# The end of the first attention and the first expert unit: blocks made as the values come, six products in another order

## The chip, the cores and the metric

The kernel runs on one core of one Trainium2 chip. The metric is the device time of one execution in microseconds (us). A core has TensorE (PE, with its weight loads shown apart as PEld), VectorE (DVE), ScalarE (ACT), GpSimd (POOL) and SyncE (SP, which here issues most of the DMAs). Each engine works through its own queue in order; semaphores tie the queues together. [...]

## The reference

```python
# attention: B=4, H=8, S=768, D=64; n_global=8, n_local=96
scores = scale * np.matmul(q, k.transpose(0, 1, 3, 2))
rel = pos[:, None] - pos[None, :]
keep = is_global | ((rel >= 0) & (rel < n_local))
scores = np.where(keep, scores - slopes * dist, -1e9)
a = softmax(scores)
attn_out = np.matmul(a, v)
# mixture: N = B*S = 3072 rows, model width 512, E=4 experts, F=1024
x = attn_out.transpose(0, 2, 1, 3).reshape(B * S, H * D)
p = domain_probs / (domain_probs.sum(-1, keepdims=True) + 1e-09)
for e in range(E):
    h = np.maximum(x @ w1[e], 0.0)
    out += p[:, e:e + 1] * (h @ w2[e])
```

All is fp32.

## The kernel before

**Precision.** A number is split into a high part, rounded to the fast matmul type, and a low part, the rest. A product is then three matmuls: high by high, low by high, high by low. The high part is mostly a ScalarE copy (`high`), the low part a subtraction on VectorE or GpSimd (`rest`).

**The mixture.** Its work is cut into units: for each of the 4 batches, 4 experts and 4 groups of 256 hidden columns, so 16 units in a batch. A unit has a first half, `first(i)` (x times w1), and a second half, `second(i)` (h times w2, six row tiles of 128, summed up over the units in `acc`). The first half multiplies 2x2 blocks by a scheme with seven products instead of eight (Winograd's form of Strassen): the weights give A11, A12, A22 and the sums S1 to S4, and x gives B11, B21, B22 and the sums T1 to T4. B11 and B12 are the first and second 384 rows of the first half of the model width, B21 and B22 those of the second half; a block spans two of the four pairs of heads (k = 0, 1 and k = 2, 3). T3 = B22 - B12, T2 = T3 + B11, T1 = B22 - T2, T4 = B21 - T2, made in place in x. Each product is six matmuls of 128x384 (two halves of the depth, three of high and low) into one PSUM tile `pm` of a pool of four. The results are joined by VectorE additions; ScalarE takes the relu as the high part of h and VectorE makes the low part (`late`, `work_late`).

**The attention.** Four pairs of heads per batch, in the order 0, 2, 1, 3, each with six row tiles of 128. One yield of `attention` is a step: the scores of one tile, the softmax of the tiles before, the turn (four transposes) of the third last, and after every third tile `weigh`, the px product with the values, whose result ScalarE copies to x. In the first batch these steps are numbered n = 0 to 27: scores come in steps 0 to 23, the last turn is in step 26, and x gets its halves of a pair in steps 6 and 9 (pair 0), 12 and 15 (pair 2), 18 and 21 (pair 1), 24 and 27 (pair 3).

**Chores.** Weights are loaded and prepared by generators that are moved one piece on after each step (`work_chores`). `load_w1` issues a load to the one buffer raw1, waits `lead` pieces, lets GpSimd make the four sums, waits `hold` pieces, and then makes four slices, a ScalarE copy and a GpSimd subtraction each. `load_w2` does the same in two slices without sums. In the first batch `keep` writes the prepared weights to DRAM, and later batches fetch them from there. `blocks` makes the B and T blocks of x, in steps too: for k = 0 during the first attention from step 17 on (pairs 0 and 2), with the low parts on GpSimd, and for k = 1 (pairs 1 and 3) after it.

**Order.** While `Ordered.on` is true, each engine's instructions stand in the order in which the program emits them. That holds for the first attention and, until `done == ONSTEPS`, for the first half of unit 0. After that a planner, which weighs costs and due times, sets the order on each engine, and the next batch's attention is spread between the units' pieces.

Of the kernel before, what the change touches and what calls it, by code (L numbers as in the profile page):

```python
# [18 lines left out]
P = 128  # L19
# [6 lines left out]
def f32(ap):  # L26
    return ap.bitcast(F32)
# [158 lines left out]
def attn_moe_kernel(ctx: ExitStack, tc, q, k, v, n_global, n_local, domain_probs, w1, w2, out):  # L186
# [25 lines left out]

    BIASES = ((0, 1), (0, 3), (1, 0), (1, 2))

    ONSTEPS = 7

    PL = P + NGLOB
    fast = main.enter_context(tc.tile_pool(name="fast", bufs=1))
# [75 lines left out]
    def mixture():  # L294

        sy.dma_start(prob, domain_probs.rearrange("(t p) e -> p t e", p=P))
        yield
        psumm = fast.tile([P, NT, 1], F32, name="psumm")
        ve.reduce_sum(psumm, prob, axis=AX.X)
        ve.tensor_scalar_add(psumm, psumm, 1e-9)  # L300
        ve.reciprocal(psumm, psumm)
        for e in range(E):
            ve.tensor_mul(prob[:, :, e : e + 1], prob[:, :, e : e + 1], psumm)
# [176 lines left out]
    xs = {}  # L480
# [116 lines left out]
    def blocks(b, ks=(0, 1), low=ve):  # L597

        lo, hi = ks[0], ks[-1] + 1
        b11, b12 = xs[b][:, lo:hi, :HALF], xs[b][:, lo:hi, HALF:]
        b21, b22 = xs[b][:, 2 + lo : 2 + hi, :HALF], xs[b][:, 2 + lo : 2 + hi, HALF:]

        def high(name, src):
            if lo == 0:
                xb[name] = bp.tile([P, 2, 2, HALF], F32R, name=f"x{name}")
            ac.copy(xb[name][:, 0, lo:hi], src)

        def rest(eng, name, src):  # L610
            eng.tensor_tensor(xb[name][:, 1, lo:hi], src, f32(xb[name][:, 0, lo:hi]), op=ALU.subtract)

        high("B11", b11)
        high("B22", b22)
        ve.tensor_sub(b12, b22, b12)
        rest(po, "B22", b22)
        yield 1
        rest(low, "B11", b11)
        ve.tensor_add(b11, b12, b11)
        high("T2", b11)  # L620
        yield 1
        rest(low, "T2", b11)
        ve.tensor_sub(b22, b22, b11)
        high("T1", b22)
        yield 1
        rest(low, "T1", b22)
        high("T3", b12)
        yield 1
        rest(po, "T3", b12)
        high("B21", b21)  # L630
        ve.tensor_sub(b11, b21, b11)
        yield 1
        rest(po, "B21", b21)
        high("T4", b11)
        yield 1
        rest(low, "T4", b11)
        yield 1


    NPR = FF // (2 * P)  # L640
    units = [(b, e, g) for b in range(B) for e in range(E) for g in range(NPR)]
# [7 lines left out]
    def keep(i, n):  # L649

        if (i, n) in waiting:
            key, dst = waiting.pop((i, n))
            kept[key] = dp.tile(list(dst.shape), F32R, name="kept_{}_{}_{}".format(*key))
            sy.dma_start(f32(kept[key]), f32(dst))
# [6 lines left out]
    def load_w1(i, wait=0, lead=5, hold=2):  # L661


        if i >= len(units):
            return
        b, e, g = units[i]
        if b > 0:
            wts[(i, 1)] = fetch("w1s", (e, g, 1), [P, 2, 7, 2, P], lambda t: {
                name: t[:, :, n] for n, name in enumerate(("A11", "A12", "A22", "S1", "S2", "S3", "S4"))
            })  # L670
            return
        for _ in range(wait):
            yield 1
        raw = rp.tile([P, KT, 2 * P], F32, name="raw1")
        sy.dma_start(raw, w1[e, :, g * 2 * P : (g + 1) * 2 * P].rearrange("(a p) f -> p a f", p=P))
        for _ in range(lead):
            yield 1
        a11, a21 = raw[:, 0:2, :P], raw[:, 0:2, P:]
        a12, a22 = raw[:, 2:4, :P], raw[:, 2:4, P:]
        sums = rp.tile([P, 4, 2, P], F32, name="sums")  # L680
        s1, s2, s3, s4 = (sums[:, n] for n in range(4))
        po.tensor_add(s1, a21, a22)
        po.tensor_sub(s2, s1, a11)
        po.tensor_sub(s3, a11, a21)
        po.tensor_sub(s4, a12, s2)
        for _ in range(hold):
            yield 1
        dst = wp.tile([P, 2, 7, 2, P], F32R, name="w1s")
        wts[(i, 1)] = {name: dst[:, :, n] for n, name in enumerate(("A11", "A12", "A22", "S1", "S2", "S3", "S4"))}
        for sl, src in (  # L690
            (slice(0, 2), raw[:, :, :P].rearrange("p (n a) f -> p n a f", n=2)),
            (slice(2, 3), a22.rearrange("p (n a) f -> p n a f", n=1)),
            (slice(3, 5), sums[:, 0:2]),
            (slice(5, 7), sums[:, 2:4]),
        ):
            ac.copy(dst[:, 0, sl], src)
            po.tensor_tensor(dst[:, 1, sl], src, f32(dst[:, 0, sl]), op=ALU.subtract)
            yield 1
        waiting[(i, 1)] = (e, g, 1), dst

    def load_w2(i, lead=7):

        if i >= len(units):
            return
        b, e, g = units[i]
        if b > 0:
            wts[(i, 2)] = fetch("w2s", (e, g, 2), [P, 2, 2, DM], lambda t: t)
            return
        raw = rp.tile([P, 2, DM], F32, name="raw2")
        sy.dma_start(raw, w2[e, g * 2 * P : (g + 1) * 2 * P, :].rearrange("(a p) m -> p a m", p=P))  # L710
        for _ in range(lead):
            yield 1
        dst = wp.tile([P, 2, 2, DM], F32R, name="w2s")
        wts[(i, 2)] = dst
        for f in range(2):
            ac.copy(dst[:, 0, f], raw[:, f])
            po.tensor_tensor(dst[:, 1, f], raw[:, f], f32(dst[:, 0, f]), op=ALU.subtract)
            yield 1
        waiting[(i, 2)] = (e, g, 2), dst

    hs = {}

    def product(i, a, x):

        pm = ps_mm.tile([P, 512], F32, name="pm")
        m = 0
        for kt in range(2):
            for wi, xi in ((0, 0), (1, 0), (0, 1)):
                te.matmul(
                    pm[:, :HALF], wts[(i, 1)][a][:, wi, kt, :], xb[x][:, xi, kt, :], start=(m == 0), stop=(m == 5)  # L730
                )
                m += 1
        return pm
# [3 lines left out]
    def work_late():  # L737

        while late:
            lo, src, hi = late.pop()  # L740
            ve.scalar_tensor_tensor(lo, src, 0.0, f32(hi), op0=ALU.max, op1=ALU.subtract)

    def first(i):

        h = hp.tile([P, 2, 2, S], F32R, name="h")
        hs[i] = h

        def relu(f, c, src):
            hi, lo = h[:, 0, f, c * HALF : (c + 1) * HALF], h[:, 1, f, c * HALF : (c + 1) * HALF]
            ac.activation(hi, src, AF.Relu)  # L750
            late.append((lo, src, hi))

        def add(out, pm, other):
            ve.tensor_add(out, pm[:, :HALF], other)
            work_late()

        def last(pm, other):

            add(pm[:, :HALF], pm, other)
            return pm[:, :HALF]  # L760

        p1, u, vv = (up.tile([P, HALF], F32, name=n) for n in ("p1", "u", "vv"))
        keep(i, 1)
        pm = product(i, "A11", "B11")
        ac.copy(p1, pm[:, :HALF])
        yield
        add(u, product(i, "S2", "T2"), p1)
        yield
        add(vv, product(i, "S1", "T1"), u)
        yield  # L770
        pm = product(i, "S3", "T3")
        add(u, pm, u)
        relu(1, 1, last(pm, vv))
        yield
        relu(0, 0, last(product(i, "A12", "B21"), p1))
        yield
        relu(0, 1, last(product(i, "S4", "B22"), vv))
        yield
        relu(1, 0, last(product(i, "A22", "T4"), u))
        yield  # L780
# [33 lines left out]
    def work_chores():  # L814
        for c in list(chores):
            if next(c, 0) == 0:
                chores.remove(c)

    bp = main.enter_context(tc.tile_pool(name="bp", bufs=1))
    Ordered.on = True  # L820
    with ExitStack() as start_stack:
        A = Pools(start_stack, "start", st=1, kd=2, qd=2, nat=2, natv=3, pb=4, ps=2, pt=3, px=1, early=True)
        for n, _ in enumerate(attention(0, A, early=True)):
            if n == 9:
                chores += [load_w1(0, lead=2), load_w2(0, lead=3)]
            if n == 18:
                chores.append(load_w1(1, lead=2, hold=3))
            if n == 2 * NQT + 5:
                chores.append(blocks(0, (0,), po))
            work_chores()  # L830
        mix = mixture()
        next(mix)
    Ordered.on = False
    hp = main.enter_context(tc.tile_pool(name="hp", bufs=2))
    up = main.enter_context(tc.tile_pool(name="up", bufs=1))
    op = main.enter_context(tc.tile_pool(name="op", bufs=1))
    ps_mm = main.enter_context(tc.tile_pool(name="ps_mm", bufs=4, space=PSUM))
    A = Pools(main, "att", st=1, kd=1, qd=1, nat=1, natv=1, pb=2, ps=2, pt=2, px=0, early=False)
# [3 lines left out]
    per = E * NPR  # L842
    count, span = NPAIR * (6 + NQT) + 5, (13 * per - 12) * 0.97
    Ordered.on = True
    chores.append(blocks(0, (1,)))
    for _ in range(2):
        work_chores()
    for b in range(B):
        att = attention(b + 1, A) if b + 1 < B else iter(())
        emitted = done = 0  # L850
# [67 lines left out]
```

## Time and profile before

| | |
|---|---|
| runs | 1203.69 us median of 3 (1201.08 to 1203.73) |
| profiled execution | 1202.66 us |
| its span, first to last instruction | 1200.9 us |
| mean granted PE clock | 0.993 |
| busy: PE, DVE, ACT, POOL | 1174.0, 824.1, 494.7, 210.7 us |
| first attention's last px product ends | 68.69 us |
| unit 0's second half starts on PE | 87.97 us |

Rows of the profile name tiles with buffer numbers left out: ps are scores, pb probabilities, pt transposes, px the weighted values, pm the products of the mixture, xB and xT the blocks B and T, w1s and w2s the prepared weights. All these instructions stand under one line, 42, because one helper emits them, so they are told apart by tile. An arrow from an engine and tile behind a row names what ended the idle time before it.

### The profile page before, as it was taken

Reading aid. Unit: us, or ns where it says so; the run is one execution under the profiler, and the core shown is the slowest. Engines: PE = TensorE matmul, PEld = TensorE weight load, DVE = VectorE, ACT = ScalarE, POOL = GpSimd, SP = SyncE. Lnnn points to the kernel's source line nnn. Section 1 sums busy time; section 2 is a strip of 40 time slices with the busy share of each in tenths; the row PEclk is TensorE's granted clock in tenths of the full one; section 3 lists DMA queues with packets and bytes.
Section 4 is the critical chain, followed back from the end, with each engine's and each line's share of the span. In section 5 each row is a group of like instructions: output and inputs, shape, how many; then the busy total and the mean of one; then the engine's idle time right before and its main releaser. Section 6 shows DMA issues by size and latency. Waiting matters only on the chain.

```text
span 1200.9 us, 18119 instructions
## 1 busy us (share of the span) xinstructions
PE 1174.0 (98%) x6624; PEld 1045.0 (87%) x6624; DVE 824.1 (69%) x1858; ACT 494.7 (41%) x1268; POOL 210.7 (18%) x222
## 2 busy tenths in 40 slices
PE   7889999999999999999999999999999999999997
PEld 5677889989889989989888989989898999999996
DVE  7776567667678767676668767676666766666665
ACT  6865655565643444444342434444443211111110
POOL 4645655645440000000002000000000000000000
PEclk9899999999999999999999999999999999999999
DMA  7456777787878567565746757574663655544532
GB/s 169 119 198 214 259 288 245 288 292 234 325 253 265 191 198 239 187 220 176 240 169 205 248 186 228 196 231 163 219 206 132 245 194 193 187 178 181 190 132 90
DMA packets 122704, 251.39 MB, mean 209 GB/s; under 512 B 83184, under 2 KB 91376, under 8 KB 106224
## 3 DMA queue, kind: packets, MB, share of 16 engines
q1 hardware_dynamic: 118864, 243.87, 61.1%
q10 hardware_dynamic: 3744, 6.30, 1.4%
q8 instruction: 54, 0.88, 0.3%
q14 instruction: 42, 0.34, 0.1%
HBM read 174.11 MB, written 52.43 MB: 189 GB/s over the span
## 4 chain that ended last, share of the span: by engine, by line
PE 88%; DMA 3%; ACT 2%; issue 2%; POOL 2%; DVE 1%; SPq 1%; POOLq 0%; ACTq 0%; DVEq 0%
PE pm L42 77%; PE pt L42 7%; PE ps L42 4%; DMA raw<-in_moe_w_dram 2%; POOL sums L42 1%; PE px L42 1%; POOL w2s L42 1%; ACT pb L42 1%; SPq L42 1%; DMA qd<-st_q 1%; DMA q<-in_q_dram 0%; ACT xT L42 0%; DVE x L42 0%; ACT xB L42 0%; ACT h L42 0%
## 5 line engine op out<-in xcount | busy, mean ns | idle before, releaser
L42 PE MATMUL pm<-w2s,h 128*128 128x512 f32 x2304 | 551.7, 393 | 4.5 <-DVE h L42 4.5
L42 PEld LDWEIGHTS pm<-w2s,h 128*128 128x128 f32 x2304 | 426.1, 188 | 92.5 <-DVE h L42 6.3
L42 DVE SCALAR_TENSOR_TENSOR acc<-pm,prob,acc 128x512 f32<-128x512 f32 x360 | 268.2, 749 | 148.8 <-PE pm L42 146.5
L42 PE MATMUL pm<-xT,w1s 128*128 128x384 f32 x1536 | 296.7, 338 | 0.2 <-ACT xT L42 0.2
L42 PEld LDWEIGHTS pm<-xT,w1s 128*128 128x128 f32 x1536 | 267.8, 189 | 2.5 <-issue 1.4
L42 PE MATMUL pm<-xB,w1s 128*128 128x384 f32 x1152 | 226.8, 338 | 1.8 <-DVE xB L42 1.5
L42 PEld LDWEIGHTS pm<-xB,w1s 128*128 128x128 f32 x1152 | 201.3, 188 | 7.0 <-DVE xB L42 1.8
L42 ACT ACTIVATE h<-pm 128x384 fp32r<-128x384 f32 x256 | 124.8, 491 | 177.7 <-DVE pm L42 174.3
L42 DVE SCALAR_TENSOR_TENSOR h<-pm,h 128x384 fp32r<-128x384 f32 x256 | 140.9, 552 | 13.1 <-ACT h L42 9.5
L42 ACT ACTIVATE pb<-pb,nmax 128x256 f32<-128x256 f32 (+1 forms) x192 | 93.1, 487 | 95.3 <-DVE nmax L42 94.6
L42 ACT COPY p<-pm 128x384 f32<-128x384 f32 x64 | 30.7, 479 | 191.1 <-PE pm L42 182.0
L42 POOL COPY vg<-v 32x768 f32<-32x768 f32 x16 | 13.2, 828 | 498.6 <-DMA v<-in_v_dram 435.9
L42 DVE TENSOR_TENSOR u<-pm,p 128x384 f32<-128x384 f32 x64 | 35.6, 556 | 73.4 <-PE pm L42 53.5
L42 DVE CUSTOM_DVE_ANT_0 pb<-ps,nbias 128x256 f32<-128x256 f32 (+1 forms) x192 | 71.7, 397 | 10.5 <-PE ps L42 5.7
L42 ACT COPY pT<-pt 128x512 f32<-128x512 f32 (+1 forms) x96 | 52.6, 548 | 58.1 <-PE pt L42 57.8
L42 DVE TENSOR_TENSOR pm<-pm,vv 128x384 f32<-128x384 f32 x128 | 71.7, 560 | 1.6 <-PE pm L42 1.4
L42 ACT ACTIVATE pb<-pb,zsum 128x256 f32<-128x256 f32 (+1 forms) x144 | 63.3, 485 | 18.0 <-DVE zsum L42 18.0
L42 PE MATMUL pt<-ident,pb 128*128 128x128 f32 x352 | 58.3, 283 | 2.7 <-DVE pb L42 1.5
L42 PEld LDWEIGHTS pt<-ident,pb 128*128 128x128 f32 x352 | 42.2, 143 | 15.4 <-ACT pb L42 3.6
L42 DVE TENSOR_TENSOR vv<-pm,u 128x384 f32<-128x384 f32 x64 | 35.7, 557 | 27.1 <-PE pm L42 26.2
L42 DVE TENSOR_TENSOR u<-pm,u 128x384 f32<-128x384 f32 x64 | 35.7, 557 | 25.1 <-PE pm L42 24.4
L42 POOL TENSOR_TENSOR w2s<-raw,w2s 128x512 fp32r<-128x512 f32 x32 | 41.0, 1296 | 57.6 <-ACT w2s L42 57.6
(88 smaller groups left out, 887.3 us busy)
## 6 DMA issues: line engine op xcount, KB each, us to landing
w1s<-kept SPq DMA_DIRECT2D x48, 1792.0 KB, 7.4
w2s<-kept SPq DMA_DIRECT2D x48, 1024.0 KB, 4.9
kept<-w1s SPq DMA_DIRECT2D x16, 1792.0 KB, 9.5
qd<-st_q SPq DMA_DIRECT2D x96, 192.0 KB, 4.7
raw<-in_moe_w_dram SPq DMA_DIRECT2D x32, 512.0 KB, 5.6
kept<-w2s SPq DMA_DIRECT2D x16, 1024.0 KB, 6.7
v<-in_v_dram SPq DMA_DIRECT2D x16, 384.0 KB, 3.4
out_dram<-acc ACTq DMA_DIRECT2D x24, 256.0 KB, 3.9
```

The lines of the kernel that those rows point to most:

```text
L42: ins = fn(*args, **kwargs)
```

## The change

- Step 9 begins w1 and w2 of unit 0 as before, but w2's two slices come in steps 14 and 15 instead of 12 and 13.
- w1 of unit 1 begins in step 17 instead of 18 and is held one step less: its slices come in steps 21 to 24 instead of 23 to 26.
- The blocks for k = 1 come from a new generator, `last_blocks`. B11 is split after step 19 (its low part on GpSimd), B21 after step 26 (on VectorE); after the attention come B22, T2, T1, T3, T4, with all low parts but T3's on VectorE. Before, B21's and B22's were GpSimd's too.
- Unit 0's first product, A11·B11, is issued after step 25, into a PSUM tile of the scores' pool (`opening`), and its result is copied to p1. `keep`, the write of unit 0's w1 to DRAM, goes with it.
- The other six products of unit 0 come in the order A12·B21, S4·B22, S2·T2, S1·T1, S3·T3, A22·T4. S4·B22 stays in its PSUM tile until S1·T1 has been added. Before, it was A11·B11, S2·T2, S1·T1, S3·T3, A12·B21, S4·B22, A22·T4.
- `ONSTEPS` is 6 instead of 7, as unit 0's first half has one piece less. After the attention one round of chores runs before unit 0 instead of two.

```diff
-    ONSTEPS = 7
+    ONSTEPS = 6
...
+    def last_blocks():
+        b11, b12, b21, b22 = (
+            xs[0][:, k : k + 1, s] for k in (1, 3) for s in (slice(0, HALF), slice(HALF, S))
+        )
+        def high(name, src):
+            ac.copy(xb[name][:, 0, 1:2], src)
+        def rest(eng, name, src):
+            eng.tensor_tensor(xb[name][:, 1, 1:2], src, f32(xb[name][:, 0, 1:2]), op=ALU.subtract)
+        high("B11", b11)
+        rest(po, "B11", b11)
+        yield 1
+        high("B21", b21)
+        rest(ve, "B21", b21)
+        yield 1
+        high("B22", b22)
+        ve.tensor_sub(b12, b22, b12)
+        ve.tensor_add(b11, b12, b11)
+        rest(ve, "B22", b22)
+        high("T2", b11)
+        rest(ve, "T2", b11)
+        yield 1
+        ve.tensor_sub(b22, b22, b11)
+        high("T1", b22)
+        rest(ve, "T1", b22)
+        yield 1
+        high("T3", b12)
+        rest(po, "T3", b12)
+        yield 1
+        ve.tensor_sub(b11, b21, b11)
+        high("T4", b11)
+        rest(ve, "T4", b11)
+        yield 1
...
+    def opening(A):
+        ups.append(sums_of_products())
+        keep(0, 1)
+        pm = product(0, "A11", "B11", A.ps.tile([P, 512], F32, name="ps0"))
+        ac.copy(ups[0][0], pm[:, :HALF])
...
+        if i == 0:
+            p1, u, vv = ups.pop()
+            relu(0, 0, last(product(i, "A12", "B21"), p1))
+            yield
+            pm4 = product(i, "S4", "B22")
+            yield
+            add(u, product(i, "S2", "T2"), p1)
+            yield
+            add(vv, product(i, "S1", "T1"), u)
+            relu(0, 1, last(pm4, vv))
+            yield
+            pm = product(i, "S3", "T3")
+            add(u, pm, u)
+            relu(1, 1, last(pm, vv))
+            yield
+            relu(1, 0, last(product(i, "A22", "T4"), u))
+            yield
+            return
...
             if n == 9:
-                chores += [load_w1(0, lead=2), load_w2(0, lead=3)]
-            if n == 18:
-                chores.append(load_w1(1, lead=2, hold=3))
+                chores += [load_w1(0, lead=2), load_w2(0, lead=5)]
             if n == 2 * NQT + 5:
-                chores.append(blocks(0, (0,), po))
+                chores += [load_w1(1, lead=2, hold=2), blocks(0, (0,), po)]
             work_chores()
+            if n == 3 * NQT + 1:
+                last = last_blocks()
+                next(last)
+            if n == 4 * NQT + 1:
+                opening(A)
+            if n == 4 * NQT + 2:
+                next(last)
...
-    chores.append(blocks(0, (1,)))
-    for _ in range(2):
-        work_chores()
+    chores.append(last)
+    work_chores()
```

More of the change, by code (lines that the diff above doesn't have):

```diff
@@ L721, in attn_moe_kernel, with product @@
     hs = {}
-    def product(i, a, x):
-        pm = ps_mm.tile([P, 512], F32, name="pm")
+    def product(i, a, x, pm=None):
+        if pm is None:
+            pm = ps_mm.tile([P, 512], F32, name="pm")
         m = 0
@@ L741, in work_late, with sums_of_products @@
             ve.scalar_tensor_tensor(lo, src, 0.0, f32(hi), op0=ALU.max, op1=ALU.subtract)
+    ups = []
+    def sums_of_products():
+        return [up.tile([P, HALF], F32, name=n) for n in ("p1", "u", "vv")]
+    def opening(A):
[3 more added lines that the diff above has]
+        ac.copy(ups[0][0], pm[:, :HALF])
     def first(i):
@@ L760, in last @@
             return pm[:, :HALF]
-        p1, u, vv = (up.tile([P, HALF], F32, name=n) for n in ("p1", "u", "vv"))
+        if i == 0:
[16 more added lines that the diff above has]
+            return
+        p1, u, vv = sums_of_products()
         keep(i, 1)
@@ L819, in attn_moe_kernel @@
     bp = main.enter_context(tc.tile_pool(name="bp", bufs=1))
+    up = main.enter_context(tc.tile_pool(name="up", bufs=1))
     Ordered.on = True
@@ L834, in attn_moe_kernel @@
     hp = main.enter_context(tc.tile_pool(name="hp", bufs=2))
-    up = main.enter_context(tc.tile_pool(name="up", bufs=1))
     op = main.enter_context(tc.tile_pool(name="op", bufs=1))
```

## The prediction

> **What bounds the kernel now.** I read the page's busy times first, then busy times by stretch of time. In each stretch row stand the length, the busy time of PE (with instruction count), PEld, DVE, ACT and POOL, the granted PE clock, the DMA share and GB/s.
>
> ```profile
> span 1200.9 us, 18119 instructions
> PE 1174.0 (98%) x6624; PEld 1045.0 (87%) x6624; DVE 824.1 (69%) x1858; ACT 494.7 (41%) x1268; POOL 210.7 (18%) x222
> ...
> 0.00:73.00 73.00, 59.88 (x418) 39.73 (x418) 52.83 (x291) 55.15 (x166) 41.59 (x57) 0.93 0.50 131
> 73.00:100.00 27.00, 25.19 (x125) 22.67 (x126) 20.85 (x44) 10.21 (x23) 12.52 (x13) 0.94 0.71 215
> 100.00:130.00 30.00, 27.09 (x147) 24.28 (x147) 18.23 (x47) 17.98 (x48) 19.52 (x20) 1.00 0.88 302
> 160.00:200.00 40.00, 38.02 (x215) 34.60 (x216) 25.48 (x58) 24.57 (x65) 26.68 (x28) 1.00 0.81 273
> ```
>
> TensorE is the bound: it idles 26.9 us in all, 13.1 of them before 73 us (the first attention and its end, which the change edits) and 6.7 in the three later stretches shown (1.8, 2.9, 2.0). Whatever makes the expert stage begin earlier ends the program earlier by as much, unless a later gap grows.
>
> **Part 1, w2's preparation two steps later.** Times next to steps (one step is one yield of the first attention, some 1.8 us) come from the timelines: start, duration, engine, instruction, idle time before it and its releaser.
>
> ```profile
> 34.37 0.52 ACT L42 ACTIVATE early_q<-pt 128x384 f32<-128x384 f32 x1
> 37.13 0.62 ACT L42 CAST w2s<-raw 128x512 fp32r<-128x512 f32 x1 [2.24 <-DMA raw<-in_moe_w_dram]
> ...
> 36.01 0.73 POOL L42 TENSOR_TENSOR sums<-raw 128x256 f32<-128x256 f32 x1 [6.91 <-DMA raw<-in_moe_w_dram]
> ...
> 39.05 0.55 PE L42 MATMUL pt<-ident,k 128*128 128x128 f32 x3 [1.95 <-ACT pT L42]
> ...
> 39.00:44.00 5.00, 4.95 (x36) 3.51 (x36) 3.34 (x23) 5.00 (x16) 4.35 (x5) 0.66 0.07 28
> 44.00:48.00 4.00, 3.79 (x25) 2.40 (x24) 3.20 (x19) 4.00 (x13) 3.18 (x4) 1.00 0.96 323
> ```
>
> At step 12 ScalarE reaches w2's first copy 2.24 us before w2 has landed. Everything behind it in ACT's queue stands, the exponentials of the attention first, and then PE (1.95 idle). Afterwards ACT is full (5.00 of 5, 4.00 of 4): it sets the pace. With lead=5 the copy comes at step 14, some 3.5 us later in ACT's order, and w2 is there. The next ACT copy from DRAM data is then w1's at step 13, about 36.5 us; POOL's wait ends at 36.01, when w1 has landed, so no new stall. Gain 2.2 us; the bounds are 0 (another engine takes over as pace) and 2.24.
>
> The moved halves now lie deeper in POOL's queue, ahead of the block halves of step 17.
>
> ```profile
> 38.87 1.27 POOL L42 TENSOR_TENSOR w2s<-raw,w2s 128x512 fp32r<-128x512 f32 x1
> 49.50 1.97 POOL L42 TENSOR_TENSOR xB<-x,xB 128x384 fp32r<-128x384 f32 x2 [1.01 <-ACT xB L42]
> ...
> 43.25 0.39 PE L42 MATMUL px<-pT,v 128*64 128x128 f32 x4
> ...
> L42 POOL TENSOR_TENSOR w1s<-sums,w1s 128x512 fp32r<-128x512 f32 x4 | 5.1, 1278 | 1.0 <-ACT w1s L42 1.0
> L42 POOL TENSOR_TENSOR xT<-x,xT 128x384 fp32r<-128x384 f32 x4 | 4.0, 1002 | 3.1 <-ACT xT L42 3.1
> L42 POOL TENSOR_TENSOR w1s<-raw,w1s 128x256 fp32r<-128x256 f32 x2 | 1.5, 732 | 0.9 <-ACT w1s L42 0.9
> L42 POOL COPY vg<-v 32x768 f32<-32x768 f32 x1 | 0.8, 820 | 0.7 <-POOL w2s L42 0.7
> ...
> 51.49 0.56 DVE L42 TENSOR_TENSOR x<-x 128x384 f32<-128x384 f32 x1 [0.83 <-POOL xB L42]
> ...
> 52.32 0.98 PE L42 MATMUL ps<-early_k,early_q 64*128 64x256 f32 x4 [1.05 <-DVE nmax L42]
> ...
> 56.00:60.00 4.00, 4.00 (x29) 3.22 (x30) 3.93 (x20) 2.21 (x9) 3.78 (x5) 0.50 0.02 6
> ```
>
> POOL is done with w1's sums at 38.87. The copy of v's window waits for the px product of step 15, which ends at 43.25 + 0.39 = 43.64 and 2.4 us earlier in the changed kernel, at 41.2 (the stall gone, the clock warmer); before that wait fit early_k and w1's first low half. Then vg 0.82 (42.0), w1's half of 256 columns 0.73, and two halves of w1 and two of w2 at 1.28 each: 5.1, so 47.8. The two block halves of 1.0 end at 49.8, against 51.47 before. VectorE's sum of the blocks, which waits for them (0.83 idle now) and holds all of VectorE's softmax, moves from 51.49 to 49.8: 1.7 us of the 2.2 is left. PE's gap of 1.05 becomes some 1.5, and the low clock after it (0.50 in the last row) I take as unchanged.
>
> **Part 2, w1 of unit 1 a step earlier and held a step less.** Its four slices go from steps 23 to 26 to steps 21 to 24. ACT is again full at the end:
>
> ```profile
> 66.03 0.42 ACT L42 CAST w1s<-raw 128x256 fp32r<-128x256 f32 x1
> 66.82 0.64 ACT L42 CAST w1s<-sums 128x512 fp32r<-128x512 f32 x1
> ...
> 66.37 0.86 PE L42 MATMUL pt<-ident,pb 128*128 128x128 f32 x4 [0.91 <-DVE pb L42]
> 68.30 0.39 PE L42 MATMUL px<-pT,v 128*64 128x128 f32 x4
> ```
>
> Two slices stood behind the last exponentials (step 24) and now stand before them. Starts to next starts, the small one takes 0.31 (66.03 to 66.34) and the large one 0.52 (66.82 to 67.34): the last tile's softmax is 0.8 later against its surroundings, so 0.9 of the 1.7 is left. The copy of B11 of pair 1 (0.5, step 19) is taken up by ACT's idle time before 60 us (2.21 busy of 4). The last px product, which ends at 68.69 now, ends at 67.8. The load's place in SP's queue counts for nothing, since SP issues it once raw1 is free.
>
> **Part 3, A11·B11 amid the transposes.** Six matmuls take some 1.1 us (below). The product goes between the last two turns, where PE waits 0.91; the last tile's probabilities come 0.8 later by part 2, so 0.1 to 0.2 at most lies on the path; I take 0.1 (67.9). ACT's copy of p1 (0.5) replaces slices that have left. The write of w1s to DRAM moves to step 25, into a stretch like the last one above (DMA share 0.02): nothing; where it stood before it met other loads.
>
> **Part 4, the new order of unit 0.**
>
> ```profile
> 68.62 0.79 PE L42 MATMUL pm<-xB,w1s 128*128 128x384 f32 x3
> 71.78 0.44 PE L42 MATMUL pm<-xB,w1s 128*128 128x384 f32 x1 [1.49 <-DVE xB L42]
> 72.92 4.68 PE L42 MATMUL pm<-xT,w1s 128*128 128x384 f32 x15 [0.17 <-ACT xT L42]
> 77.44 2.27 PE L42 MATMUL pm<-xB,w1s 128*128 128x384 f32 x12
> 79.55 1.30 PE L42 MATMUL pm<-xT,w1s 128*128 128x384 f32 x6
> 87.97 2.93 PE L42 MATMUL pm<-w2s,h 128*128 128x512 f32 x12
> ...
> L42 DVE TENSOR_TENSOR x<-x 128x384 f32<-128x384 f32 x4 | 3.3, 822 | 2.7 <-ACT x L42 2.6
> L42 DVE TENSOR_TENSOR xT<-x,xT 128x384 fp32r<-128x384 f32 x3 | 1.7, 552 | 0.6 <-ACT xT L42 0.6
> L42 DVE TENSOR_TENSOR xB<-x,xB 128x384 fp32r<-128x384 f32 x1 | 1.3, 1343 | 0.0
> ...
> 80.74 0.55 DVE L42 SCALAR_TENSOR_TENSOR h<-pm,h 128x384 fp32r<-128x384 f32 x1
> 81.20 0.56 DVE L42 TENSOR_TENSOR pm<-pm,u 128x384 f32<-128x384 f32 x1
> ```
>
> Now: px ends at 68.69 and unit 0's second half starts at 87.97, 19.3 us for 84 matmuls. At the full rate (12 in 2.11, from 77.44 to 79.55: 0.176 each) they take 14.8; the rest is waits (1.49 and smaller) and a slow stretch of 15 in 4.52 instead of 2.64.
> After: 78 matmuls remain, 13.7 us if nothing waits. The wait is now VectorE's: a 128x384 operation follows the next in 0.47 (80.74 to 81.20). From px's end as zero: x copied 0.53; b12 and b11 0.55 to 1.58; B22's low half till 2.06; T2's till 2.7. PE does A12·B21 at once (B21 was made a step before), begins S4·B22 at 1.05, waits some 0.5 for the low half, ends at 2.8, S2·T2 at 3.9. T1's low half comes behind the sum for A12·B21 and the subtraction for T1, at 4.8: S1·T1 ends at 5.5, S3·T3 at 6.6; T4's low half is there at 7.3, A22·T4 ends at 8.0. S4·B22's buffer is held until VectorE, with the two sums and T4 before it, has made its low half at 9.3. Unit 1 then runs as buffers come free, products starting at 8.0, 9.3, 10.9, 11.9, 13.0, 14.1, 15.1: the second half starts at 16.2. The bounds are 13.7 and 19.3; I take 16.2 because VectorE has as many operations as before. T3's low half (1.0, still on POOL) meets some of them. The x and xB rows show such meetings: 0.82 and 1.34 instead of 0.55. I add 0.4: 16.6, a gain of 2.7.
>
> [...]
>
> **Sum.** 0.8 (67.9 for 68.69) + 2.7 = 3.5 us at the start of the second half. Beyond it I take the gaps as they are. ONSTEPS shifts the next attention's 53 pieces by one step in some 190, no cost. The profiled execution took 1202.66 (its span 1200.9); less 3.5 is 1199.2. The median 1203.69 lies 1.0 above that execution, inside the runs' 1201.08 to 1203.73; I keep 1199.2.
>
> **Rivals.**
>
> ```profile
> 95.45 0.55 PE L42 MATMUL pt<-ident,q 128*128 128x128 f32 x3 [1.81 <-DVE st_q L42]
> ...
> 45.21 0.38 SPq L42 DMA_DIRECT2D raw<-in_moe_w_dram  x1
> ...
> 30.23 6.87 DMA raw<-in_moe_w_dram
> ```
>
> Rival 1, given back (no change). From 88 us on instructions are unordered and the planner sets them anew; w2(1) and w1(2) are prepared after the same count of pieces, so a piece later against PE. For it: the gap of 1.81 and the other gaps, 6.7 together, come from preparation. Against it: POOL idles for over a third of these stretches. If they grow by half, 3.3, nothing is left: 1202.5.
>
> Rival 2, slower. Place: w1(1)'s sums on POOL at step 19, now ahead of T2's low half. They wait for the raw load, whose issue at 45.21 moves with raw1's release to about 42.7 and lands, at 6.87, at 49.6: just in time for 49.8. If SP first issues w2's write, free only after w2's new place (about 46.5), the load lands at 53.5, T2's low half ends at 57.4 instead of 53.6, and VectorE's next block subtraction (step 21, about 55.5) stands 1.9 with the softmax behind it. It decides from a landing of 51.7 on, each us costing one; the loss passes the whole gain of 3.5 at a landing of 55.2. With a landing of 59, 3.8 later still, the time is 1206.5.
>
> Rival 3, more gain. If the gap at 52 us doesn't bring the low clock, PE's 56 to 60 stretch (4.00 busy at 0.50) takes half: 2 us more, 1197.2. Against it: the gap gets longer.
>
> **Chances.** Forecast 0.42, rival 3 0.10 (both faster, 0.52); rival 1 0.38; rival 2 or a worse plan behind it 0.10. About 0.3%, 3.6 us, is what a measurement can tell from no change: my point lies 4.5 below the median, close to that edge, which is why no change keeps 0.38. The forecast's own range is 1197.8 to 1200.5; the range for 8 in 10 goes from rival 3 with a little more from part 4 (13.7 instead of 16.6), 1196, to rival 1 with the runs' spread, 1203.2.
>
> **What would show it.** Right: no ACT wait for w2's load near 35 us; the block sum near 50; six pm matmuls between the last two turns; A12·B21 within 0.3 us of px's end near 68; the clock near 1.00 in the five us after it; the second half's first matmul near 84.5; gaps of about 6.7 from 73 to 200. Wrong: a wait of POOL's sums for the load near 50 with VectorE standing, the px end at 68.5 or later, a PE wait of over 1 us for T1, T4 or a buffer, or gaps from 88 on of over 9 us.

## The result and the profile after

| | before | after |
|---|---|---|
| runs, median of 5 each | 1201.32 us (1199.57 to 1203.73) | 1192.06 us (1189.79 to 1196.28) |
| ratio after to before, 95% interval | | 0.9921 (0.9902 to 0.994) |
| profiled span | 1200.9 us | 1190.3 us |
| TensorE busy + idle in it | 1174.0 + 26.9 us | 1168.9 + 21.4 us |
| of the idle: to 64 us, 64 to 100, 100 to 200 | 10.3, 4.7, 4.9 us | 10.8, 3.4, 0.0 us |

The change gained 9.3 us of median, where 3.5 were forecast. The page of the changed kernel and its busy times by stretch (columns as in the prediction):

```profile
span 1190.3 us, 18101 instructions
...
PE 1168.9 (98%) x6624; PEld 1041.2 (87%) x6624; DVE 826.3 (69%) x1859; ACT 495.0 (42%) x1268; POOL 211.1 (18%) x221
...
0.00:73.00 73.00, 60.73 (x443) 41.66 (x444) 56.62 (x298) 56.84 (x170) 46.23 (x62) 0.98 0.65 185
...
100.00:130.00 30.00, 30.00 (x165) 26.80 (x165) 21.24 (x51) 19.41 (x52) 17.18 (x18) 1.00 0.91 316
...
160.00:200.00 40.00, 40.00 (x231) 36.07 (x230) 27.64 (x65) 24.95 (x67) 22.11 (x23) 1.00 0.81 273
```

The same matmuls (x6624) keep TensorE busy 5.1 us less: they ran at a higher clock (0.997 in the mean of this execution, 0.993 in that of the kernel before), as shown below. And TensorE idles 5.5 us less: the gaps behind 100 us, 1.82 and 1.98 the largest in the kernel before, are gone (30.00 of 30, 40.00 of 40). Those two gaps, in the timeline of the kernel before:

```profile
128.73 3.06 PE L42 MATMUL pm<-w2s,h 128*128 128x512 f32 x12 [1.82 <-DVE h L42]
170.18 5.74 PE L42 MATMUL pm<-w2s,h 128*128 128x512 f32 x24 [1.98 <-DVE h L42]
```

**The clock.** First the stretches of the kernel before with a low clock (56 to 60 stands in the prediction), then the changed kernel us by us around the only low spell before 200 us, and the stretch behind its last px product:

```profile
36.00:40.00 4.00, 2.05 (x14) 1.23 (x13) 1.40 (x10) 2.87 (x9) 3.91 (x5) 0.96 0.04 11
40.00:44.00 4.00, 4.00 (x33) 2.81 (x29) 2.38 (x16) 4.00 (x14) 3.35 (x5) 0.61 0.08 35
...
52.00:56.00 4.00, 3.68 (x12) 2.15 (x12) 3.93 (x29) 3.63 (x12) 2.28 (x3) 0.67 0.00 0
...
72.00:76.00 4.00, 3.83 (x15) 3.00 (x15) 2.46 (x6) 2.23 (x5) 1.03 (x2) 0.73 1.08 437
76.00:80.00 4.00, 4.00 (x21) 4.00 (x21) 3.61 (x7) 1.29 (x3) 0.93 (x1) 0.84 1.08 362
```

```profile
42.00:43.00 1.00, 0.20 (x2) 0.01 (x1) 0.28 (x3) 1.00 (x5) 1.00 (x2) 1.00 0.81 228
43.00:44.00 1.00, 0.52 (x3) 0.35 (x3) 0.96 (x6) 1.00 (x4) 1.00 (x2) 1.00 0.86 294
44.00:45.00 1.00, 1.00 (x4) 0.58 (x4) 1.00 (x3) 1.00 (x5) 1.00 (x2) 0.52 0.01 2
45.00:46.00 1.00, 1.00 (x9) 0.89 (x10) 0.96 (x9) 1.00 (x4) 1.00 (x1) 0.50 0.62 262
46.00:47.00 1.00, 1.00 (x14) 1.00 (x12) 0.84 (x4) 1.00 (x5) 1.00 (x2) 0.50 0.93 393
47.00:48.00 1.00, 1.00 (x10) 0.41 (x6) 0.00 (x0) 0.86 (x2) 1.00 (x2) 0.77 0.97 393
...
68.00:72.00 4.00, 2.83 (x13) 2.17 (x13) 3.42 (x7) 1.90 (x4) 1.15 (x2) 1.00 0.95 281
```

A stretch loses its length times what its clock lacks of 1; an unbroken run of low clock is called a spell here. The changed kernel loses 0.48 + 0.50 + 0.50 + 0.23 = 1.7 us, one spell of 3.4 us at half clock. The kernel before loses 1.7 between 36 and 44 us, 3.3 between 52 and 60 (0.67, and 0.50 in the row of the prediction) and 1.7 between 72 and 80: four such spells, 6.8 us with the last tenth at 60. Three spells fewer are 5.1 us, as much as TensorE's busy time fell by. That is one execution of each. The mean clock over the timed executions is 0.9945 for the kernel before (91 executions, the four series of experiments) and 0.9962 for the changed one (5 executions), a difference of 2.0 us in 1195, so the clock's share of the median's gain is nearer 2 than 5 us.

The count leaves out the start of the program. The records show 1.00 there, yet the four matmuls of a tile's scores take 1.23 us at 17.85 in the kernel before and 0.70 at 17.32 in the changed one: TensorE came to its full pace earlier in that execution, and the first px product starts at 19.87 instead of 21.01. No edit stands ahead of it.

**Around the change.** The changed kernel's timeline, TensorE, then VectorE, then GpSimd:

```profile
61.46 0.86 PE L42 MATMUL pt<-ident,pb 128*128 128x128 f32 x4
62.07 1.31 PE L42 MATMUL ps<-xB,w1s 128*128 128x384 f32 x6
63.22 0.86 PE L42 MATMUL pt<-ident,pb 128*128 128x128 f32 x4
...
65.18 0.39 PE L42 MATMUL px<-pT,v 128*64 128x128 f32 x4
65.50 2.18 PE L42 MATMUL pm<-xB,w1s 128*128 128x384 f32 x11
69.17 0.44 PE L42 MATMUL pm<-xB,w1s 128*128 128x384 f32 x1 [1.48 <-DVE xB L42]
69.45 5.24 PE L42 MATMUL pm<-xT,w1s 128*128 128x384 f32 x24
74.70 1.32 PE L42 MATMUL pm<-xB,w1s 128*128 128x384 f32 x6
...
86.19 5.74 PE L42 MATMUL pm<-w2s,h 128*128 128x512 f32 x24 [0.71 <-DVE h L42]
```

```profile
48.16 1.07 DVE L42 TENSOR_TENSOR x<-x 128x384 f32<-128x384 f32 x1 [1.32 <-POOL xB L42]
66.13 1.98 DVE L42 TENSOR_TENSOR x<-x 128x384 f32<-128x384 f32 x2
68.04 1.07 DVE L42 TENSOR_TENSOR xB<-x,xB 128x384 fp32r<-128x384 f32 x1
```

```profile
64.95 1.74 POOL L42 TENSOR_TENSOR sums<-raw 128x256 f32<-128x256 f32 x2
...
67.78 0.92 POOL L42 TENSOR_TENSOR sums<-raw,sums 128x256 f32<-128x256 f32 x1
```

The last px product ends at 65.57 instead of 68.69. Unit 1's first product (the 74.70 row) comes 9.1 us after that; before it was 80.69 - 68.69 = 12.0:

```profile
80.69 1.21 PE L42 MATMUL pm<-xB,w1s 128*128 128x384 f32 x6
```

Unit 0's second half starts at 86.19, 20.6 after px instead of 19.3, as pieces of the next attention now stand in front of it.

### The profile page after: what moved, and what is told of

Its sections match the earlier page's. It is cut to its first block, busy times and chain, and to the rows that moved or that the text cites. A ratio compares the mean times of both kernels' runs of the same rounds, so it can differ in the third digit from the quotient of the medians.

```text
span 1190.3 us, 18101 instructions
## 1 busy us (share of the span) xinstructions
PE 1168.9 (98%) x6624; PEld 1041.2 (87%) x6624; DVE 826.3 (69%) x1859; ACT 495.0 (42%) x1268; POOL 211.1 (18%) x221
## 4 chain that ended last, share of the span: by engine, by line
PE 93%; DVE 2%; DMA 2%; ACT 1%; POOL 1%; issue 0%; SPq 0%; DVEq 0%; POOLq 0%
PE pm L42 81%; PE pt L42 8%; PE ps L42 4%; DMA qd<-st_q 1%; PE px L42 1%; DVE x L42 0%; POOL w1s L42 0%; ACT pb L42 0%; DMA q<-in_q_dram 0%; ACT xT L42 0%; POOL w2s L42 0%; ACT xB L42 0%; ACT w1s L42 0%; POOL xB L42 0%; DVE h L42 0%
## 5 line engine op out<-in xcount | busy, mean ns | idle before, releaser
L42 DVE SCALAR_TENSOR_TENSOR h<-pm,h 128x384 fp32r<-128x384 f32 x256 | 140.4, 551 | 10.8 <-ACT h L42 7.5
```

The costliest lines, as they stand in the source:

```text
L42: ins = fn(*args, **kwargs)
```

## The experiments

Ratios are to the kernel before, measured on the same chip in the same series (its median 1201.6 to 1202.0), with 95% intervals. 0.1% is 1.2 us. "Later gaps" is TensorE's idle time from 100 to 200 us; "lost clock" is counted as above, to 84 us. Both are from one profiled execution.

### The parts one by one

**w2 alone**, in the kernel before:

```diff
-                chores += [load_w1(0, lead=2), load_w2(0, lead=3)]
+                chores += [load_w1(0, lead=2), load_w2(0, lead=5)]
```

> The kernel before with w2's slices of unit 0 in steps 14 and 15, nothing else. Theory 'stall': the 2.2 us wait of ScalarE near 35 us goes and with it PE's low clock from 39 to 43 us, so the last px product ends 2 to 3 us earlier and the time falls by 2 to 3 us, the PE gaps from 88 to 200 us staying near 6.7. Theory 'plan' (the gaps after 88 us come anew with every new plan, whatever was changed): the gaps there may be anything from 0 to 8, so the time may move by -9 to +3 us. Theory 'raw1' (the gaps go only where the buffer raw1 comes free earlier for unit 2's w1): gaps stay at 5 to 8 us here.

0.9953 (0.9937 to 0.9969). Its stretches, TensorE's largest late gap, and VectorE ahead of it:

```profile
44.00:48.00 4.00, 3.78 (x27) 2.86 (x28) 3.38 (x16) 3.87 (x14) 4.00 (x4) 0.58 1.04 261
52.00:56.00 4.00, 3.93 (x39) 2.62 (x38) 3.93 (x24) 3.79 (x14) 3.92 (x5) 1.00 0.02 6
68.00:72.00 4.00, 3.85 (x14) 3.34 (x13) 2.20 (x5) 2.23 (x5) 1.39 (x2) 0.57 0.99 401
```

```profile
165.47 5.74 PE L42 MATMUL pm<-w2s,h 128*128 128x512 f32 x24 [2.00 <-DVE h L42]
```

```profile
161.46 0.17 DVE L42 RECIPROCAL zsum<-zsum 128x2 f32<-128x2 f32 x1 [2.39 <-ACT zsum L42]
163.24 1.12 DVE L42 TENSOR_TENSOR kd<-pt,kd 64x384 fp32r<-64x384 f32 x2 [0.67 <-ACT kd L42]
```

A part forecast at 1.7 to 2.2 us brought about 5.6. Two low spells are gone (52 to 56 is at 1.00), 3.4 us of lost clock in place of 6.8; over the timed executions the mean clock is 0.9967 against 0.9947 for the kernel before in the same series, 2.4 us. The later gaps stayed (4.8).

**w1 of unit 1 alone**, and **both loads** (this and w2's line):

```diff
-            if n == 18:
-                chores.append(load_w1(1, lead=2, hold=3))
             if n == 2 * NQT + 5:
-                chores.append(blocks(0, (0,), po))
+                chores += [load_w1(1, lead=2, hold=2), blocks(0, (0,), po)]
```

> The kernel before with w1 of unit 1 begun in step 17 and held one step less, nothing else. Theory 'raw1': unit 2's load of w1 is issued near 60 us instead of 71, its sums are done some 10 us earlier, and the PE gaps from 88 to 200 us fall from 6.7 to under 2.5: time 4 to 6 us lower, though the px end is no earlier (within 1 us). Theory 'plan': gaps no smaller on average than in the other kernels. The prediction on record: 0.8 us worse.

> The kernel before with both changes of the loads, blocks and products as before. Theories 'stall' and 'raw1' together: 6 to 8 us lower than before, that is most of the change's 9.4. If the gain comes mostly from the new order of the products and the clock there: 2 to 4 us lower only.

w1 alone: 1.0026 (1.0014 to 1.0038), 3.1 us slower where 0.8 was forecast. Both: 0.9985 (0.9973 to 0.9996). So on top of w2 it costs 0.32%, 3.8 us. Either way its profile has three spells of low clock in the first attention (5.2 us lost), and more between 100 and 120 us: two with w1 alone (3.5 us), one with both loads (1.8).

**The changed kernel with w1 of unit 1 as before.** One theory of the vanished gaps was that raw1 comes free earlier.

```diff
+            if n == 18:
+                chores.append(load_w1(1, lead=2, hold=3))
             if n == 2 * NQT + 5:
-                chores += [load_w1(1, lead=2, hold=2), blocks(0, (0,), po)]
+                chores.append(blocks(0, (0,), po))
```

> The changed kernel with w1 of unit 1 again begun in step 18, after the blocks, and held three pieces. Theory 'raw1': PE gaps from 88 to 200 us of 4 us or more come back, time 4 to 6 us above the changed kernel (1196 to 1198 where that has 1192). Theory 'order' (the new order of the products brings the most): within 2 us of the changed kernel.

0.9916 (0.99 to 0.9933), later gaps 0.7. Within the changed kernel w1's earlier place is worth nothing that the time shows. The theory is hardly put to the test: the load of unit 2's w1 was issued at 61.43 here and at 59.60 in the changed kernel, and with w1 alone in the kernel before at 69.86, where that has 70.94. Runs further down settle it.

**A11·B11 behind the last px product** instead of amid the transposes:

```diff
-            if n == 4 * NQT + 1:
+            if n == 4 * NQT + 3:
                 opening(A)
```

> The changed kernel with A11*B11 issued after the last px product instead of amid the last transposes. The prediction's step: the product's 1.1 us moves into the path, but VectorE sets the pace there, so 0 to 1.1 us slower than the changed kernel. If the product amid the transposes is what keeps PE's clock up through unit 0: clock under 0.8 in the five us after the px end, 2 to 3 us slower.

0.992 (0.9904 to 0.9935), no lost clock behind 64 us. The place of this product amid the transposes is worth nothing that can be measured.

**The old order of products** in the changed kernel, with all loads and the early B11 and B21 kept (unit 0 then goes the common way of `first`):

```diff
-    ONSTEPS = 6
+    ONSTEPS = 7
...
-        if i == 0:
-            p1, u, vv = ups.pop()
...
-            return
...
-            if n == 4 * NQT + 1:
-                opening(A)
```

> The changed kernel with the six plus one products of unit 0 in their old order after the attention (seven pieces, ONSTEPS 7), while the loads and the early halves of B11 and B21 stay as in the change. Theory 'products' (the new first unit sets what follows): low clock after the px end, PE gaps of 3 to 5 us from 100 to 200 us, time 6 to 8 us above the changed kernel, near that of the kernel with both loads alone (1200). Rival 'blocks' (B11 and B21 early bring it): within 2 us of the changed kernel's 1192.

0.9978 (0.9965 to 0.9991): 0.57%, 6.8 us, above the changed kernel. A spell of low clock stands between 100 and 110 us (1.7 us). Later gaps 3.9, the larger of them:

```profile
102.36 1.98 PE L42 MATMUL pm<-w2s,h 128*128 128x512 f32 x6 [2.94 <-DVE h L42]
162.44 5.74 PE L42 MATMUL pm<-w2s,h 128*128 128x512 f32 x24 [1.53 <-DVE h L42]
```

Against both loads alone (0.9985) the early blocks brought little: the intervals overlap.

**The clock at the transition by itself**: the kernel before with 14 transposes ahead of unit 0 into a tile that nobody reads.

```diff
+        if i == 0:
+            idle = ps_mm.tile([P, 512], F32, name="pm")
+            for n in range(14):
+                te.transpose(idle[:, n % 4 * P : (n % 4 + 1) * P], ident, ident)
```

> The kernel before with 14 idle transposes on PE ahead of A11*B11, where PE waits for the blocks; their result is not used. It prices the low clock by itself. If the clock is lowered because PE idles there: clock near 1.0 in the eight us after the px end instead of 0.7 to 0.8, unit 1 starts 1 to 2 us earlier, time 1 to 2 us below before. If VectorE sets the pace anyway: clock up, time within 0.7 us of before.

0.9956 (0.994 to 0.9972). With TensorE fed, 64 to 80 us runs at 1.00, against 1.7 us lost there before. But the later gaps fell too, to 1.6, although nothing of the products' order was touched. That pointed to what the planner does behind 88 us as a thing of its own. (The extra tile also shifts which of the four pm buffers each later product gets, which was not told apart.)

### What closes the later gaps

In w2's run above, the zsum of a softmax stands at 161.46 in VectorE's queue, between the sums of a first half, and waits 2.39 for ScalarE; kd follows at 163.24. Low halves of h behind them come late, and TensorE waits 2.00 at 165.47. In the changed kernel the same zsum stands ahead of the sums:

```profile
152.08 0.17 DVE L42 RECIPROCAL zsum<-zsum 128x2 f32<-128x2 f32 x1 [0.97 <-ACT zsum L42]
153.32 0.56 DVE L42 TENSOR_TENSOR u<-pm,p 128x384 f32<-128x384 f32 x1 [1.08 <-PE pm L42]
```

In this one gap, then, it is the place of a piece of the next attention among the unit's pieces that makes TensorE wait. What moves such pieces could be `ONSTEPS`, the order of products, their number of pieces, or the piece at which the preparations fall.

**ONSTEPS alone**, 6 in the kernel before, 6 on top of w2 later, and 7 in the changed kernel:

```diff
-    ONSTEPS = 7
+    ONSTEPS = 6
```

> The kernel before with ONSTEPS = 6 and nothing else: the load of unit 2's w1, issued at the seventh piece, is no longer in the fixed order, so the planner may put it ahead of the write of unit 1's w1 on SyncE's queue. Theory 'load freed': unit 2's sums come near 71 us instead of 90, the PE gaps from 100 to 200 us fall from 4.9 to under 1.5, time 3 to 5 us below before. Theory 'products' (the gaps vanish because unit 0 ends earlier and in another order): gaps stay at 4 to 5, time within 1.5 us of before.

> The kernel before with w2's slices later (which alone gave 0.9953) and ONSTEPS = 6, no new blocks, no new order of products. If both are additive: about 0.991 to 0.993, that is as fast as the whole change, and the new blocks and the new order bring under 2 us. If the new order carries the rest: about 0.995.

> The changed kernel with ONSTEPS = 7, so that the order stays fixed for one piece of unit 1 and with it the load of unit 2's w1. Theory 'load freed': the write of unit 1's w1 stands ahead of that load again, gaps of 3 to 5 us from 100 to 200 us return, time 3 to 5 us above the changed kernel (about 1195 to 1197). Theory 'products': no gaps, time within 1.5 us of the changed kernel.

0.9989 (0.9978 to 1.0), gaps 3.2; 0.9973 (0.9963 to 0.9982), gaps 3.2; 0.9903 (0.9886 to 0.992), gaps 0.0. In the old order ONSTEPS takes 1.6 to 1.7 us of the gaps off, not all, and isn't needed in the changed kernel. On top of w2 later it still costs 2.4 us (0.9973 against 0.9953): the mean clock is 0.9942 against 0.9967. In the first of these kernels unit 2's raw w1 was issued at 65.38, ahead of 70.94, and GpSimd's sums of it began at 69.76, with 3.2 us of gaps left; on top of w2 they began at 66.55, with 3.2 too. In the changed kernel with ONSTEPS 7 they began only at 73.37, and there are no gaps. So an earlier load isn't the cause.

**Preparation shifted by one piece**, one earlier and one later in the changed kernel, and one later on top of w2 later:

```diff
-                chores += [load_w2(1, 12), load_w1(2, 6, 3)]
+                chores += [load_w2(1, 13), load_w1(2, 7, 3)]
```

> The changed kernel with the preparations of unit 1's w2 and unit 2's w1 one piece earlier, so that they stand to unit 1 as in the kernel before. Theory 'phase' (the gaps from 100 to 200 us hang on which piece these preparations fall): gaps of 3 to 5 us return, 3 to 5 us slower than the changed kernel. Theory 'products': gaps stay under 1 us, time within 1.5 us of the changed kernel.

> The changed kernel with the preparations of unit 1's w2 and unit 2's w1 one piece later (one piece earlier gave 1196.1, 4 us slower). It tells the scatter of the plan: theory 'order': gaps from 100 to 200 us stay under 1.2, but with stalls before 100 us and the clock the time may lie anywhere from 1189 to 1197.

> The kernel before with w2's slices later, and with the preparations of unit 1's w2 and unit 2's w1 one piece later, so that they stand to unit 1 as in the changed kernel. Theory 'phase': the gaps from 100 to 200 us (4.8 with w2's slices later alone) fall under 1.5, time near 1193. Theory 'products': gaps stay at 3 to 5, time 1196 to 1199.

Earlier (11 and 5): 0.995 (0.9934 to 0.9967). Later: 0.9927 (0.9914 to 0.994). Later with w2 only: 1.0 (0.9984 to 1.0016), against 0.9953 without the shift. One piece moves the time by up to 5.6 us, as much as most parts of this change. With the shift on top of w2 the later gaps sum to 4.5 us, no more than the 4.8 without it, but at another place:

```profile
106.78 2.93 PE L42 MATMUL pm<-w2s,h 128*128 128x512 f32 x6 [2.93 <-DVE h L42]
```

What makes it slower is the clock: its mean over 12 runs is 0.9925, against 0.9967 without the shift, which is 5.0 us of 1200. The changed kernel with the piece earlier is 3.5 us slower at the same mean clock, 0.9962. Its profile shows 1.0 us of later gaps; the rest stays open.

**Order against number of pieces.** The new order with an empty seventh piece and ONSTEPS 7; and the kernel with w2 later, its old order put in six pieces (A11·B11 and S2·T2 in one), ONSTEPS 6, and a third round of chores ahead of unit 0.

```diff
     # new order, seven pieces
-    ONSTEPS = 6
+    ONSTEPS = 7
...
             relu(1, 0, last(product(i, "A22", "T4"), u))
             yield
+            yield
             return
```

```diff
     # old order, six pieces
-    ONSTEPS = 7
+    ONSTEPS = 6
...
-        yield
+        if i:
+            yield
...
-                chores += [load_w1(0, lead=2), load_w2(0, lead=3)]
+                chores += [load_w1(0, lead=2), load_w2(0, lead=5)]
...
-    for _ in range(2):
+    for _ in range(3):
```

> The changed kernel with an empty seventh piece at the end of unit 0's first half and ONSTEPS 7, so that pieces and preparations stand to unit 1 as in the kernel before. Theory 'order' (the new order itself takes the later gaps away, as VectorE's work on unit 0 is done earlier): PE gaps from 100 to 200 us under 1.2, time 1189 to 1194. Theory 'pieces' (the shift by one piece does): gaps of 3 to 5 us, time 1195 to 1198.

> The kernel before with w2's slices later, and with unit 0 in its old order but in six pieces (A11*B11 and S2*T2 in one), ONSTEPS 6 and three rounds of block chores ahead of it. Theory 'order': gaps from 100 to 200 us stay at 3 to 5, time 1196 to 1200. Theory 'pieces': gaps under 1.2, time about 1192 to 1194.

New order in seven: 0.9942 (0.9929 to 0.9955), later gaps 0.00. Old order in six: 0.9957 (0.9945 to 0.997), later gaps 0.03. The stretches of the latter:

```profile
68.00:72.00 4.00, 3.37 (x8) 2.14 (x8) 2.57 (x3) 1.82 (x5) 2.09 (x4) 0.55 0.97 401
72.00:76.00 4.00, 2.73 (x9) 2.54 (x9) 2.43 (x4) 0.33 (x1) 2.26 (x2) 0.50 0.99 296
76.00:80.00 4.00, 4.00 (x18) 4.00 (x17) 2.95 (x6) 1.38 (x3) 0.00 (x0) 0.67 1.17 313
...
100.00:200.00 100.00, 99.97 (x585) 90.60 (x584) 68.14 (x159) 62.88 (x163) 60.24 (x62) 1.00 0.82 282
```

So either of the two goes with closed gaps, and neither is needed: of the old order in seven pieces eight kernels have 3.2 to 4.9 us (the one with transposes 1.6), of the other three combinations all have 0 to 1.0. The old order in six pieces also has ONSTEPS 6 and a round of chores more, so the number of pieces was not changed alone. Which feature of the plan closes the gaps stays open. The old order in six pieces is no faster than w2 alone (0.9953), although 4.8 us of gaps are gone: its three spells between 68 and 80 lose 5.1 us, against 1.7 there, and over the timed executions its mean clock is 0.9929 against 0.9967, 4.6 us. And the new order in seven waits 3.29 us for kd ahead of its second half, at 85.16.

**Two of these edits together**: the changed kernel with ONSTEPS 7 and w1 of unit 1 as before (the two diffs above).

> The changed kernel with ONSTEPS 7 and with w1 of unit 1 begun in step 18 as before. If the two add: px ends near 63 us as in the kernel with the latter alone, and the time is 1187 to 1189, the fastest here. If the plan decides: 1188 to 1194.

0.9892 (0.9878 to 0.9907), 1188.71 us: the fastest version, below both kernels. Its interval still touches that of the changed kernel (0.9902 to 0.994).

### The stretches in all eighteen profiles

One profile can mislead. The first attention of the kernel before is the same code in the kernels with the transposes and with ONSTEPS 6 alone, and its last px product ended at 68.69, 65.12 and 67.14. From the start of the first px product, which leaves the start of the program out, to the end of the last, the first attention took:

| first attention | profiles | us |
|---|---|---|
| as before | 3 | 46.97 to 47.68, mean 47.3 |
| w2 later | 4 | 43.77 to 45.35, mean 44.4 |
| w2 later, w1 of unit 1 earlier | 1 | 47.0 |
| as in the changed kernel | 5 | 45.70 to 46.80, mean 46.3 |
| the same, w1 of unit 1 as before | 2 | 44.35 and 44.99, mean 44.7 |

So w2 later takes 2.9 us off, w1 of unit 1 earlier gives 1.6 to 2.6 back, and 1.0 is left for the change. From the end of the last px product to unit 1's first product it is:

| order of unit 0's products | profiles | us |
|---|---|---|
| old, with low clock between 64 and 84 us | 6 | 11.8 to 16.4 |
| old, without | 2 | 10.8 |
| old, B11 and B21 early, without | 1 | 9.4 |
| new | 8 | 8.0 to 10.3 |

(The one with transposes has 11.6.) The 12.0 of the kernel before became 9.1. By these few profiles most of that is the missing spell (10.8) and the early B11 and B21 (9.4); the new order, with A11·B11 ahead, adds 0.3 in the changed kernel and 1.3 at best within unit 0. In time it brings far more: with ONSTEPS 7 in both, it is 0.9903 against 0.9978 for the old one, 9.0 us, and with an empty seventh piece as well 0.9942, 4.3 us. So the greater part of what the new order brings lies behind unit 0, 3.9 us of it in the later gaps.

## Why the prediction was wrong

The direction was right and the point 7.1 us too high. Of this, 1.3 lie in what it was counted from, an execution of 1202.66, where the median of the kernel before came out at 1201.32. The rest by its own steps:

- **w2 later.** The wait at 35 us is gone, and VectorE's sum of the blocks, due at 49.8, came at 48.16, after 1.32 us of waiting for GpSimd: the chain through GpSimd's queue held. The step that failed is "the low clock after it I take as unchanged". With w2 later the first attention has 1, 1, 2 and 1 spells in its four profiles, as before 3, 2 and 2, and it is 2.9 us shorter, not 1.7. That was rival 3, given 0.10, with its price of 2 us for one stretch. In time the part brought 5.6 us alone, but 1.9 with ONSTEPS 6 in both kernels (0.9973 against 0.9989); what lies beyond the first attention hangs on the plan.
- **w1 of unit 1 earlier.** Forecast 0.8 us of cost. The first attention gets 2.6 longer by it in the old surroundings and 1.6 in the changed kernel, so the sum of copy times on ScalarE's queue was two to three times too small. Why was not told apart. In time it costs 3.1 to 3.8 in the old surroundings and nothing measurable in the changed kernel. Rival 2 didn't come about: unit 1's load was issued at 41.00, and GpSimd began its sums at 48.09 without a wait.
- **The px end.** Forecast 67.9, measured 65.57. Of this 3.1 us below 68.69, 1.1 lie ahead of any edit (the first px product starts at 19.87 instead of 21.01), a difference of the two executions. Over all profiles the first attention is 1.0 shorter, where 0.8 was forecast. That this fits is luck: the forecast had the gain from w2 and the cost of w1 both too small, by about the same.
- **A11·B11 amid the transposes.** Forecast 0 to 0.1, and nothing measurable was found. Six matmuls stand at 62.07 between the last two turns, as said. The write of w1s to DRAM did not go where the forecast had it: SyncE issued it at 46.24, as soon as w1s was ready.
- **The new order.** A12·B21 follows px at once (65.50) and the clock stays at 1.00, as said. The wait for B22's low half was forecast at 0.5 and is 1.48: VectorE's two sums took 1.98 us and the low half 1.07, beside GpSimd's sums for unit 2 (64.95 to 68.7), which the forecast did not place there. Before, they began at 89.70:

```profile
89.70 1.43 POOL L42 TENSOR_TENSOR sums<-raw 128x256 f32<-128x256 f32 x2
```

  In SP's queue unit 2's load now stands ahead of unit 1's write to DRAM (first the changed kernel, then the kernel before):

```profile
59.60 0.38 SPq L42 DMA_DIRECT2D raw<-in_moe_w_dram  x1
64.90 0.34 SPq L42 DMA_DIRECT2D kept<-w1s  x1
```

```profile
70.08 0.81 SPq L42 DMA_DIRECT2D kept<-w1s  x2
70.94 2.29 SPq L42 DMA_DIRECT2D raw<-in_moe_w_dram  x2
```

  With the preparation one piece earlier the changed kernel makes the same sums at 76.39, and VectorE's operations and the wait are short (TensorE, VectorE, GpSimd):

```profile
68.69 0.45 PE L42 MATMUL pm<-xB,w1s 128*128 128x384 f32 x1 [0.19 <-DVE xB L42]
66.95 1.22 DVE L42 TENSOR_TENSOR x<-x 128x384 f32<-128x384 f32 x2 [0.34 <-ACT x L42]
68.08 0.55 DVE L42 TENSOR_TENSOR xB<-x,xB 128x384 fp32r<-128x384 f32 x1
76.39 1.45 POOL L42 TENSOR_TENSOR sums<-raw 128x256 f32<-128x256 f32 x2
```

  So the term for meetings with GpSimd, 0.4, was 1.3 here (1.48 against 0.19), from work that the forecast had elsewhere. It varies: with the preparation a piece later the sums begin at 64.87 too, and the wait is 0.73. Where the sums come later, in this run, with ONSTEPS 7 and with seven pieces, unit 1's first product comes 8.0 to 8.5 after px, as in the forecast's schedule (8.0); in the changed kernel it comes 9.1 after it. (With ONSTEPS 7 and w1 of unit 1 as before it is 9.4, with a wait of 0.57 for an earlier block, B21.) In the changed kernel VectorE's low half took 1.07 us, beside GpSimd's sum of 0.92 at 67.78, and 0.55 with the preparation a piece earlier. What holds it up there was not shown.
- **The second half at 84.5.** It came at 86.19, although px ended earlier than forecast: the planner put transposes of q and k, with waits of 0.66 and 0.71, ahead of it. Those pieces then don't stand later; what that is worth on balance was not told apart.
- **"Beyond it I take the gaps as they are."** The second failing step, and the larger one: 4.9 us of gaps behind 100 us went to nothing, against a forecast of no change there (from 73 to 200 us 1.9 are left of 6.7). Rival 1 had the right mechanism (the planner sets everything behind 88 us anew) and only the sign of a loss.

A rough sum from the rows is 1.0 us in the first attention, 2.9 from there to unit 1's first product and 4.9 of later gaps, 8.8 of the median's 9.3. The forecast had 0.8, 2.7 and nothing. So it is the last term that carries the error; its size is shown, and which feature of the plan set it is not.

## What to carry to other kernels

Price a wait that TensorE sees by its length and by the low clock that may follow: a spell lost 1.7 us here, whole or not at all. The same code had two or three of them from one execution to the next, so count them over several profiles, and set the mean clock of all runs beside each comparison. Where a planner orders what follows an edit, the gaps after it are drawn anew; shift its pieces by one in both kernels and see how far that alone moves the time before a part of the change is credited or blamed. An edit that changes a queue's order also moves what stood behind it, so look for the engine on which that work now meets the new critical piece.

## What the hardware showed

- The lost clock came in whole spells. In the eighteen kernels profiled, the clock lost to 100 us comes out at 1.7, 3.4, 5.1 or 6.8 us, within 0.1: one to four spells of 3.4 us at half speed (0.50 in the changed kernel from 45 to 47 us and in the kernel before from 56 to 60).
- Which gaps bring a spell was not settled. The changed kernel's spell at 44 us follows two us with 0.20 and 0.52 busy, ahead of which TensorE was busy throughout from 30 us on, while the wait of 1.48 at 69 us is followed by none (1.00 from 68 to 100 us). The same code had it at different places: the changed kernel at 44 us; with the preparation a piece earlier, the first attention being the same, once between 43 and 47 us and once more between 60 and 64, with 1.7 us lost in each.
- All eight kernels with the new order ran from 64 to 84 us without a spell. Of nine with the old order six had one to three there (1.7 to 5.1 us lost); the three without are those with w1 of unit 1 earlier. A tenth, with the extra transposes, had none. Two of the eight have w1 of unit 1 as before, so the new order does without its earlier place.
